# Attention and gated feed-forward block: the last row tile split as 384 and 128 columns, two scale sums over 64 columns

## The chip, the cores and the metric

One core of one Trainium2 chip runs the whole program. The metric is the device time of one execution in microseconds (us). The profile's span counts from the first to the last instruction and comes out some 2 us below the device time of the same run (776.1 beside 778.0 before). Before the prediction, the kernel before had a median of 777.64 us (3 runs, 777.15 to 778.16).

## The reference, cut to what matters

```python
x = A_x                                              # 2048 x 1024, bf16
h = x + _A_ref(_layernorm(x), A_wqkv, A_wo)           # 32 heads, sliding dilated window of 8, then wo
h2 = h + _B_ref(_layernorm(h), w_gate, w_up, w_down)  # ((ln @ w_gate) * (ln @ w_up)) @ w_down, width 3584
```

Nearly all the work is matrix products. The kernel computes some of them from sums and differences of sub-blocks, in fp16, with scales taken from sums of absolute values.

## The kernel before

The change touches two places. The first is the sum over partitions from which a scale is made: a matmul with a matrix of ones adds up the 128 partitions and broadcasts the total. The right-hand operand is one column repeated 512 times, and only column 0 of the result is read.

```python
def total(self, ps=None):
    ps = ps or psum.tile([128, TC], F32, tag="mm", name="l1ps" + self.name)      # TC = 512
    nc.tensor.matmul(ps[:], lhsT=ones[:], rhs=self.rowb[:].to_broadcast((128, TC)), start=True, stop=True)
    tot = const.tile([128, 1], F32, name="tot" + self.name)
    nc.vector.tensor_copy(tot[:], ps[:, 0:1])
    ...                                                    # four small VectorE steps make the scale
```

It is called four times. The scales `d` and `gu` take a bank of their own (`ps` is None); `h1` and `h` are given a bank.

The second place is the end of the kernel: four row tiles `q` of 128 rows by 512 columns. `dprod` is 14 pairs of weight load and matmul onto a bank that already holds a partial result. `result` scales, adds and stores.

```python
for q in range(4):
    if q < 3:
        dprod(ps_y[q], q, HF["12"], fcells(down["b22"]), False)
        result(2, hs2[q], q, 1, ps_y[q], inv, p5[q])
        if q == 0:
            nc.scalar.copy(ps_x[0][:, 256:512], ps_y[3][:, 256:512])
    else:
        for ps, lo in ((ps_y[3], 0), (ps_x[0], 256)):
            dprod(ps, q, HF["12"], fcells(down["b22"]), False, lo, 256)
            result(2, hs2[q], q, 1, ps, inv, p5[q], lo, 256)
```

The last tile is done in two column groups in two banks, so that the first half is evicted and stored while TensorE computes the second.

Of the kernel before, what the change touches and what calls it, by code (L numbers as in the profile page):

```python
# [25 lines left out]
TC = 512  # L26
# [52 lines left out]
def kernel(  # L79
# [11 lines left out]
    nc = tc.nc  # L91
# [441 lines left out]
    ones = const.tile([128, 128], BF)  # L533
    nc.vector.memset(ones[:], 1.0)

    class Scale:
# [11 lines left out]
            nc.vector.tensor_copy(self.rowb[:], row[:])  # L548

        def total(self, ps=None):  # L550
            ps = ps or psum.tile([128, TC], F32, tag="mm", name="l1ps" + self.name)
            nc.tensor.matmul(ps[:], lhsT=ones[:], rhs=self.rowb[:].to_broadcast((128, TC)), start=True, stop=True)
            tot = const.tile([128, 1], F32, name="tot" + self.name)
            nc.vector.tensor_copy(tot[:], ps[:, 0:1])
            eb = const.tile([128, 1], I32, name="eb" + self.name)
            nc.vector.tensor_scalar(eb[:], tot[:].bitcast(I32), 0x7F800000, None, ALU.bitwise_and)
            nc.vector.tensor_scalar(eb[:], eb[:], float(27 << 23), None, ALU.max)
            sb = const.tile([128, 1], I32, name="sb" + self.name)
            nc.vector.tensor_scalar(sb[:], eb[:], -1.0, float(266 << 23), ALU.mult, ALU.add)
            ib = const.tile([128, 1], I32, name="ib" + self.name)  # L560
            nc.vector.tensor_scalar(ib[:], eb[:], float(12 << 23), None, ALU.subtract)
            self.s, self.inv = sb[:].bitcast(F32), ib[:].bitcast(F32)
# [200 lines left out]
    def f16(ap):  # L763
        return ap.bitcast(F16)
# [19 lines left out]
    def fcells(homes):  # L784
        return [f16(t[:, k, :]) for t in homes for k in range(NH)]

    def dprod(ps, q, lhs, rhs, fresh, lo=0, n=TC):
        for k in range(NP):
            nc.tensor.matmul(ps[:, bass.ds(lo, n)], lhsT=lhs[k][:, bass.ts(q, 128)], rhs=rhs[k][:, bass.ds(lo, n)],  # L789
                             start=(fresh and k == 0), stop=(k == NP - 1), skip_group_check=not fresh)  # L790

    def result(c, rows, t, hf, ps, sc, other, lo=0, n=TC):
        cols = bass.ds(hf * 512 + lo, n)
        nc.vector.scalar_tensor_tensor(rows[:, cols], ps[:, bass.ds(lo, n)], sc,
                                       rows[:, cols] if other is None else other[:, bass.ds(lo, n)], ALU.mult, ALU.add)
        nc.sync.dma_start(outf[bass.ds(c * TC + t * 128, 128), cols], rows[:, cols])
# [124 lines left out]
    hs2 = hss[2]  # L921
# [84 lines left out]
    down = {}  # L1006
# [28 lines left out]
    ps_x = [psum.tile([128, TC], F32, tag="mm", name=f"dx{q}") for q in range(4)]  # L1035
    ps_y = [psum.tile([128, TC], F32, tag="mm", name=f"dy{q}") for q in range(4)]
# [6 lines left out]
    for q in range(4):  # L1043
        dprod(ps_x[q], q, HA["11"], fcells(down["b11"]), True)
        if q == 1:
            scale_h.total(ps_y[3])
            inv = const.tile([128, 1], F32, name="inv_hd")
            nc.vector.tensor_tensor(inv[:], scale_h.inv, scale_d.inv, ALU.mult)
            inv = inv[:]
# [3 lines left out]
    HF = {k: [f16(a) for a in HA[k]] for k in HA}  # L1053
# [22 lines left out]
    p5 = []  # L1076
# [24 lines left out]
    for q in range(4):  # L1101
        if q < 3:
            dprod(ps_y[q], q, HF["12"], fcells(down["b22"]), False)
            result(2, hs2[q], q, 1, ps_y[q], inv, p5[q])
            if q == 0:
                nc.scalar.copy(ps_x[0][:, 256:512], ps_y[3][:, 256:512])
        else:
            for ps, lo in ((ps_y[3], 0), (ps_x[0], 256)):
                dprod(ps, q, HF["12"], fcells(down["b22"]), False, lo, 256)
                result(2, hs2[q], q, 1, ps, inv, p5[q], lo, 256)  # L1110

# [1 line left out]
_INS = ['A_x', 'A_wqkv', 'A_wo', 'B_x', 'B_w_gate', 'B_w_up', 'B_w_down']  # L1113
# [26 lines left out]
```

## Time and profile before

| | before |
|---|---|
| median of the runs | 777.64 us |
| span of the profiled run | 776.1 us |
| TensorE busy | 770.0 us, 99% |
| one sum over 512 columns, on the chain | 0.21 us |
| last tile: first matmul to end of last eviction | 773.35 - 769.61 = 3.74 us |
| end of last eviction to end of span | 776.07 - 773.35 = 2.72 us |

The chain of work that ended last is read backwards from the last instruction: what stands on it sets the end. TensorE is 86% of it, so for most of the span a matmul's slot counts in full. At the very end the chain leaves TensorE: one eviction on VectorE and one store, with nothing beside them. The prediction shows the lines. The page rounds the span to 0.1 us; where 0.1 us matters below, the end is taken to 0.01 us from the view `--windows` (776.07 here).

### The profile page before, as it was taken

How to read it: one execution, taken by the hardware profiler on the slowest of the kernel's cores; microseconds unless marked ns; L12 is line 12 of the kernel's file. 1: busy time of each engine (PE TensorE's matmuls, PEld its weight loads, DVE VectorE, ACT ScalarE, POOL GpSimd, SP SyncE). 2: the span in 40 equal slices, each digit the busy share in tenths (PEclk: the TensorE clock that was granted, in tenths of full speed). 3: DMA queues.
4: the chain of work that ended last, by engine and by line, in shares of the span. 5: the costliest groups of instructions: out<-in, count | busy, mean ns of one | idle time of the engine just before them, and what ended most of it. 6: DMA issues, size and time to landing. Idle time of an engine off the chain costs nothing.

```text
span 776.1 us, 10428 instructions
## 1 busy us (share of the span) xinstructions
PE 770.0 (99%) x3691; PEld 354.4 (46%) x3691; DVE 612.0 (79%) x782; ACT 471.6 (61%) x1021; POOL 142.5 (18%) x152
## 2 busy tenths in 40 slices
PE   9999999999999999999999999999999999999998
PEld 6444444444444444444444444444444444444444
DVE  5619999999899999999988989985553444578862
ACT  4627445323476661975869889746677776788240
POOL 0000000020000200002000001008778687600000
PEclk9999999999999999999999999999999999999999
DMA  8999693895965869877745384644332423740001
GB/s 275 272 233 222 158 285 94 250 280 151 332 223 165 262 227 248 260 234 227 242 135 194 132 296 124 156 103 110 107 94 70 109 59 105 242 138 28 0 28 55
DMA packets 183716, 134.38 MB, mean 173 GB/s; under 512 B 81136, under 2 KB 176496, under 8 KB 181616
## 3 DMA queue, kind: packets, MB, share of 16 engines
q1 hardware_dynamic: 176912, 110.12, 50.5%
q0 software_dynamic: 3584, 22.02, 8.2%
q10 hardware_dynamic: 3168, 1.57, 0.8%
q8 instruction: 29, 0.48, 0.3%
q14 instruction: 23, 0.19, 0.1%
HBM read 104.86 MB, written 22.02 MB: 163 GB/s over the span
## 4 chain that ended last, share of the span: by engine, by line
PE 86%; DVE 9%; DMA 2%; ACT 1%; SPq 1%; issue 0%; ACTq 0%; DVEq 0%
PE ps L394 18%; PE pu L394 12%; PE pg L394 12%; PE dx L789 6%; PE pz L682 6%; PE acc L628 6%; PE py L682 6%; PE px L682 6%; PE wo L515 4%; PE pv L682 3%; PE dy L789 3%; DMA x<-in_A_x_dram 1%; DVE st L181 1%; DVE h L836 1%; DMA w_qkv<-in_A_wqkv_dram 1%; PE ps L355 1%
## 5 line engine op out<-in xcount | busy, mean ns | idle before, releaser
L394 PE MATMUL ps<-lnT,w_qkv 128*128 128x512 bf16 x736 | 159.7, 379 | 0.7 <-ACT sg L307 0.7
L394 PEld LDWEIGHTS <-w_qkv 128*128 128x128 bf16 x736 | 71.9, 98 | 87.0 <-issue 1.0
L394 PE MATMUL pg<-lnT,w_wg 128*128 128x512 bf16 x448 | 105.8, 379 | 0.0
L394 PE MATMUL pu<-lnT,w_wu 128*128 128x512 bf16 x448 | 105.8, 379 | 0.0
L307 ACT CAST sg<-ps 128x512 bf16<-128x512 f32 x96 | 54.8, 590 | 51.2 <-PE ps L394 48.5
L477 DVE TENSOR_TENSOR pv<-vD,at 128x4096 bf16<-128x4096 bf16 x32 | 72.5, 2286 | 0.3
L434 DVE TENSOR_TENSOR prod<-qD,kD 128x4096 bf16<-128x4096 bf16 x32 | 72.3, 2283 | 0.1
L682 PEld LDWEIGHTS <-sw 128*128 128x128 f16 x448 | 43.8, 98 | 53.5 <-issue 0.9
L394 PEld LDWEIGHTS <-w_wu 128*128 128x128 bf16 x448 | 43.8, 98 | 52.9
L394 PEld LDWEIGHTS <-w_wg 128*128 128x128 bf16 x448 | 43.8, 98 | 52.9
L598 ACT CAST us<-pu 128x512 bf16<-128x512 f32 x56 | 33.2, 593 | 40.5 <-PE pu L394 40.4
L682 PE MATMUL px<-lnT,ws 128*128 128x512 bf16 x224 | 55.2, 379 | 0.0
L682 PEld LDWEIGHTS <-ws 128*128 128x128 f16 x336 | 32.9, 98 | 39.6
L628 PE MATMUL acc<-w_wd,gs 128*128 128x512 bf16 x224 | 48.5, 379 | 0.0
L489 POOL DMA_DIRECT2D od<-oD x4 | 2.2, 544 | 251.7 <-DVE oD L487 162.5
L663 POOL TENSOR_TENSOR sw<-ws 128x512 f16<-128x512 f16 x26 | 30.0, 1154 | 84.6 <-PE py L682 77.3
L185 ACT ACTIVATE rs<-mv,eps 128x1 f32<-128x1 f32 (+1 forms) x25 | 7.4, 297 | 53.9 <-DVE mv L182 49.0
L593 ACT CAST gs<-pg 128x512 bf16<-128x512 f32 x56 | 32.9, 587 | 10.8 <-PE pg L394 8.7
L436 DVE TENSOR_TENSOR prod<-prod 128x4096 bf16<-128x4096 bf16 x16 | 36.6, 2287 | 0.3
L543 ACT ACTIVATE junkd<-w_wd 128x512 bf16<-128x512 bf16 x56 | 34.3, 613 | 0.0
L628 PEld LDWEIGHTS <-gs 128*128 128x128 bf16 x224 | 21.9, 98 | 26.4
L699 ACT COPY py<-px 128x512 f32<-128x512 f32 x28 | 16.0, 570 | 26.3 <-PE px L682 26.3
(312 smaller groups left out, 1393.4 us busy)
## 6 DMA issues: line engine op xcount, KB each, us to landing
w_wg<-in_B_w_gate_dram SPq DMA_DIRECT2D x14, 1024.0 KB, 6.7
w_wu<-in_B_w_up_dram SPq DMA_DIRECT2D x14, 1024.0 KB, 5.6
w_wd<-in_B_w_down_dram SPq DMA_DIRECT2D x8, 896.0 KB, 8.1
w_pair<-in_B_w_gate_dram SPq DMA_DIRECT2D x14, 512.0 KB, 4.0
w_pair<-in_B_w_up_dram SPq DMA_DIRECT2D x14, 512.0 KB, 5.2
w_wo<-in_A_wo_dram SPq DMA_DIRECT2D x6, 1024.0 KB, 8.3
w_qkv<-in_A_wqkv_dram SPq DMA_DIRECT2D x5, 1024.0 KB, 10.5
kd<-sg SPq DMA_DIRECT2D x32, 144.0 KB, 3.5
```

Source lines behind the costliest of these rows:

```text
L307: nc.scalar.copy(sg[:, HB:HB + TC], ps[:])
L394: nc.tensor.matmul(ps[:], lhsT=wt[:, ko, bass.ts(j, 128)], rhs=rhs[:, ko, :], start=(ko == 0), stop=(ko == KO - 1))
L434: nc.vector.tensor_tensor(prod[:, j], qD[:], kD[:, :, o:o + SUB], ALU.mult)
L436: nc.vector.tensor_tensor(prod[:, :, 0:16], prod[:, :, 0:16], prod[:, :, 16:32], ALU.add)
L477: nc.vector.tensor_tensor(pv[:, j], vD[:, :, o:o + SUB], at[:, w, None, :].to_broadcast((128, DH, SUB)), ALU.mult)
L515: nc.tensor.matmul(ps[:], lhsT=oTs[c][:, kk, t, :], rhs=wts["wo", c, hf][:, kk, :], start=(kk == 0), stop=(kk == KO - 1))
L543: nc.scalar.activation(junk, src, ACTF.Abs, accum_out=self.l1[:, k:k + 1])
L593: nc.scalar.copy(gs[:], pg[:])
L598: nc.scalar.copy(us[:], pu[:])
L628: nc.tensor.matmul(acc[t][:], lhsT=hT[f][:, bass.ts(t, 128)], rhs=wts["wd", c, hf, b][:, j, :], start=(f == 0), stop=(f == NF - 1))
L682: nc.tensor.matmul(ps[:], lhsT=lhs[:, ko, :], rhs=rhs[:, ko, :], start=(fresh and ko == 0), stop=(ko == 3), skip_group_check=not fresh)
L789: nc.tensor.matmul(ps[:, bass.ds(lo, n)], lhsT=lhs[k][:, bass.ts(q, 128)], rhs=rhs[k][:, bass.ds(lo, n)], start=(fresh and k == 0), stop=( ...
```

## The change

It is meant to shorten two sums of which one column is used, and to shorten the eviction and the store behind the last matmul by making the last column group smaller, at no cost in matmul columns. The diff, whole:

```diff
         def total(self, ps=None):
+            n = TC if ps else 64
             ps = ps or psum.tile([128, TC], F32, tag="mm", name="l1ps" + self.name)
-            nc.tensor.matmul(ps[:], lhsT=ones[:], rhs=self.rowb[:].to_broadcast((128, TC)), start=True, stop=True)
+            nc.tensor.matmul(ps[:, 0:n], lhsT=ones[:], rhs=self.rowb[:].to_broadcast((128, n)), start=True, stop=True)
@@
             if q == 0:
-                nc.scalar.copy(ps_x[0][:, 256:512], ps_y[3][:, 256:512])
+                nc.scalar.copy(ps_x[0][:, 384:512], ps_y[3][:, 384:512])
         else:
-            for ps, lo in ((ps_y[3], 0), (ps_x[0], 256)):
-                dprod(ps, q, HF["12"], fcells(down["b22"]), False, lo, 256)
-                result(2, hs2[q], q, 1, ps, inv, p5[q], lo, 256)
+            for ps, lo, n in ((ps_y[3], 0, 384), (ps_x[0], 384, 128)):
+                dprod(ps, q, HF["12"], fcells(down["b22"]), False, lo, n)
+                result(2, hs2[q], q, 1, ps, inv, p5[q], lo, n)
```

One line is added in `total`, so source lines after it are one higher in the profiles of the changed kernel (L552 is L553 there, L794 is L795).

## The prediction

> **What bounds the kernel now.** I read the page of the kernel before first, for the engines' busy shares and the chain that ended last, then the chain piece by piece around the two places where the diff acts (the sums over `ones`, and the last row tile), then the order in time of the last seven microseconds.
>
> ```profile
> PE 770.0 (99%) x3691; PEld 354.4 (46%) x3691; DVE 612.0 (79%) x782; ACT 471.6 (61%) x1021; POOL 142.5 (18%) x152
> PEclk9999999999999999999999999999999999999999
> PE 86%; DVE 9%; DMA 2%; ACT 1%; SPq 1%; issue 0%; ACTq 0%; DVEq 0%
> ```
>
> TensorE is busy for 770.0 of 776.1 us at the full granted clock (1.000 in the list of cores), and the chain that ended last runs for 86% of its time through TensorE. So a saved TensorE issue slot is worth its own length, as long as the chain passes through it. The chain in order of time says so for both changed sums; the columns are start in us, length in us, and what:
>
> ```profile
> 390.35 1.73 PE pu L394 x8
> 392.07 0.21 PE l1psd L552
> 392.29 1.73 PE pg L394 x8
> ...
> 453.59 1.73 PE wo L834 x8
> 455.31 0.21 PE l1psgu L552
> 455.53 1.73 PE wo L834 x8
> 457.25 0.22 PE ey L552
> 457.47 1.74 PE wo L834 x8
> 459.21 0.02 issue
> 459.23 0.69 DVE h L836
> ```
>
> Each sum is one matmul of 0.21 us, directly between its neighbours, with no wait on either side. At 459.23 us the chain passes to VectorE, and it is TensorE that releases VectorE there. Until 521.81 us the chain then runs through VectorE and ScalarE, mostly.
>
> The end of the kernel, in order of time (start, length from first start to last end, engine, line, operation):
>
> ```profile
> 769.61 0.82 PE L789 MATMUL dy<-dn_b22a,hq 128*128 128x256 f16 x6
> 769.81 0.75 DVE L794 SCALAR_TENSOR_TENSOR h<-dy,inv_hd,dp 128x512 bf16<-128x512 f32 x1 [2.27 <-PE dy L789]
> ...
> 771.14 0.82 PE L789 MATMUL dx<-dn_b22a,hq 128*128 128x256 f16 x6
> 771.41 0.48 DVE L794 SCALAR_TENSOR_TENSOR h<-dy,inv_hd,dp 128x256 bf16<-128x256 f32 x1 [0.84 <-PE dy L789]
> ...
> 772.45 0.38 PE L789 MATMUL dx<-dn_b22b,kx 128*128 128x256 f16 x2
> 772.87 0.48 DVE L794 SCALAR_TENSOR_TENSOR h<-dx,inv_hd,dp 128x256 bf16<-128x256 f32 x1 [0.98 <-PE dx L789]
> 773.38 0.33 SPq L796 DMA_DIRECT2D out_dram<-h  x1
> ```
>
> The last row tile is two groups of 14 matmuls of 256 columns. After the last matmul nothing is hidden: eviction (0.48 us), issue of the store at 773.38, its landing (1.6 us from issue for the 64 KB stores), and the closing work up to 776.1. The first half's eviction and store lie beside the second half's matmuls.
>
> **What the Trainium skill says, and whether this trace agrees.** (1) TensorE: Matmul & The Clock Gate, section Back-to-back issue gap, gives N/2.4 + 2.5 ns as the isolated gap of a warm matmul of N columns, and about 81 ns at N=128 and 131 ns at N=512 for a sustained stream of weight load and matmul pairs. The trace agrees with the formula where it can be checked: 14 pairs of 512 take 769.61 - 766.59 = 3.02 us, 215.7 ns each; 14 pairs of 256 take 771.14 - 769.61 = 1.53 us, 109.3 ns each (formula 109.2). It contradicts the 131 ns. (2) Same page, Single matmul latency: (398 + N)/2.4 ns warm. The groups show 379 ns at 512, 272 at 256 and 219 at 128, as the formula says; an end of a matmul is modelled, though. (3) VectorE: DVE Perf Modes, section The TRN2 errata, charges a fixed term plus one 0.96 GHz cycle per column for an fp32 PSUM source. The slope agrees (751 - 483 = 268 ns for 256 columns, 1.047 ns each); the fixed term here is larger (215 ns against 125). (4) DMA: Bandwidth & Descriptors, Specifications: below 512 B a transfer is a read-modify-write. The new last store has 256 B rows. No isolated store of that shape is in the trace, so this stays open.
>
> **The change part by part.** The instruction order of both kernels was compared: every engine keeps the same sequence and waits; only the column counts differ. Nothing is added or moved between engines.
>
> *Two sums.* `total` without a given bank is called for the `d` and `gu` scales; the `h1` and `h` sums are given a bank and keep 512 columns. So two matmuls go from 512 to 64 columns. The formula gives 64/2.4 + 2.5 = 29 ns (an estimate from the skill's page above), but then the next pair's weight load might set the pace. What this core has shown for short pairs is in the first microseconds, at 128 columns and clock 1.00:
>
> ```profile
> 9.20 0.61 PE L349 MATMUL pt<-ident,ln 128*128 128x128 bf16 x8
> 9.65 2.11 PE L355 MATMUL ps<-lnT,w_qkv 128*128 128x128 bf16 x32
> ```
>
> Subtracting one matmul's 219 ns: (2.11 - 0.219)/31 = 61 ns per pair, and (0.61 - 0.22)/7 = 56 ns. So a pair can go at 56 ns with a 98 ns load under it; the spacing at 64 columns should lie between 29 and 61. I take 45: each sum saves 216 - 45 = 171 ns, two save 0.34 us. The first shifts everything on TensorE after 392; VectorE waits for TensorE at the `wo` additions (the longest such wait before 459 is 1.24 us), so the shift is handed over at 459.23, and from there to 521.81 VectorE carries it. A constant earlier start of all of it keeps the 0.34.
>
> *Last tile, TensorE.* Group one: 14 x (384/2.4 + 2.5) = 14 x 162.5 = 2.275 us. Group two: 13 gaps of 58 ns (my choice between 56 and 61) and one end of 219 ns = 0.973. Last result at 769.61 + 2.275 + 0.973 = 772.86. Before, worked out in the same way: 769.61 + 14 x 0.1093 + 13 x 0.1093 + 0.272 = 772.83. Cost: +0.03 us (0.00 to +0.07 for 56 to 61).
>
> *Last tile, VectorE.* The last eviction has 128 columns: 483 - 128 x 1.047 = 349 ns, saving 0.13 us on the path. The other, of 384 columns, takes 483 + 134 = 617 ns. Its group's last matmul starts at 769.61 + 13 x 0.1625 = 771.72 and ends 326 ns later, so with the 0.11 us seen today between an end and an eviction it runs from about 772.16 to 772.78. The last eviction may start at 772.90: clear by 0.12 us.
>
> *Stores.* First store issued at about 772.81 (96 KB), second at about 773.28 (32 KB) instead of 773.38; one issue takes 0.33 us, so they don't collide. From issue to landing the trace has 1.7 us for 128 KB and 1.6 for 64 KB: bytes hardly count, and I give the halved last store 0.00 (within -0.05 and +0.1).
>
> *The bank copy* on ScalarE shrinks from 256 to 128 columns, off the path (ScalarE is idle at the end): 0.
>
> Sum: -0.34 + 0.03 - 0.13 + 0.00 = -0.44 us. Because some of the handover at 459 may be lost, I take -0.40: 777.64 - 0.40 = 777.24 us.
>
> **The rivals.** *Weight loads set the pace of short matmuls.* Loads are 98 ns each; if two could not overlap, group two would be 13 x 98 + 219 = 1.49 us, the tail +0.55 - 0.13 = +0.42, and the sums would save only 2 x 118 ns = 0.24: net +0.18, 777.8 us. The skill's 81 ns lies between (13 x 81 + 219 = 1.27, tail +0.20, sums -0.27: about -0.07, 777.6). Against both: the 56 and 61 ns of the fence above.
>
> *The sums' gain doesn't arrive.* VectorE or ScalarE could be the real bound between 392 and 521, a load or transpose coming last there, so that TensorE only waits longer later. Then only the tail's -0.10 remains: 777.5 us. For it: from 459 the chain is VectorE's for 60 us, and ScalarE's conversions (busy until 458.43 before the 458.72 step) leave only 0.3 us of slack there. Against it: VectorE idles for TensorE three times just before.
>
> *The first, larger half becomes the last.* If its 617 ns eviction or its store holds up the last one, the gain of the shorter last eviction is eaten: about +0.1, 777.35 us. The worked margin of 0.12 us is thin, but positive.
>
> *Small rows.* If 256 B rows cost a read-modify-write at the end, the last landing takes perhaps 0.1 us longer (an estimate: the whole data phase of such a store is a fraction of its 1.6 us): 777.35 us.
>
> **Range and chances.** All mechanisms lie between -0.5 and +0.2 us, which is under 0.07% of the time. The three runs of before spread over 1.01 us (777.15 to 778.16), so a median of a few runs is itself uncertain by some 0.3 to 0.4 us, and more than the change is worth is noise. That gives 776.6 to 778.0 for 8 in 10. A 2% change is 15.6 us; nothing here is of that size. Faster by over 2%: 0.003; within: 0.994; slower: 0.003.
>
> **What would show each step right or wrong.** In the changed kernel's profile: the chain should show `l1psd` and `l1psgu` at 0.03 to 0.06 us instead of 0.21; the span between the start of the last 512-column group and the last eviction should grow by 0.00 to 0.07; the last eviction should be near 349 ns and the one before near 617; the store's landing should stay at 1.5 to 1.7 us; the span should fall from 776.1 to about 775.7. A spacing near 98 ns in the 128-column group would make the weight load rival right; an unchanged time of the first `pv` product near 521.81 would mean that the sums' gain was absorbed. The prediction as a whole is wrong if the time moves by more than 1 us, for example by a different settling of the transfers in the middle.

## The result, and the profile after

The changed kernel took 776.76 us (median of 5 runs, 776.52 to 777.62), the kernel before 778.16 us (5 runs, 777.15 to 778.51). The ratio is 0.9988, with a 95% interval of 0.9973 to 1.0002: the same within 2%, and no change at all is inside the interval. A ratio here is the mean time of one kernel's runs over that of the other's of the same rounds, so it is not quite the ratio of the medians that are quoted.

The profiled run's span fell from 776.1 to 774.8 us. Its page:

```profile
PE 768.9 (99%) x3691; PEld 353.5 (46%) x3691; DVE 612.0 (79%) x782; ACT 471.3 (61%) x1021; POOL 142.1 (18%) x152
...
PE 86%; DVE 9%; DMA 2%; ACT 1%; SPq 1%; issue 0%; DVEq 0%
```

What bounds the kernel is as before. The chain in order of time around the two sums (start, length, what):

```profile
391.42 0.03 PE l1psd L553
391.45 1.73 PE pg L394 x8
...
454.47 0.03 PE l1psgu L553
454.50 1.73 PE wo L835 x8
456.23 0.22 PE ey L553
...
458.20 0.69 DVE h L837
```

Each changed sum has shrunk from 0.21 to 0.03 us. `ey`, which keeps 512 columns, still takes 0.22. The `h` addition on VectorE, which started at 459.23, starts at 458.20, 1.03 us sooner. Two sums account for 0.36 us of that. The rest was there before the first of them: `l1psd` starts at 391.42 instead of 392.07, 0.65 us sooner, although nothing ahead of it was changed. I come to that below.

The end in order of time:

```profile
768.60 1.14 PE L790 MATMUL dy<-dn_b22a,hq 128*128 128x384 f16 x6
...
770.88 0.50 PE L790 MATMUL dx<-dn_b22a,hq 128*128 128x128 f16 x6
771.14 0.62 DVE L795 SCALAR_TENSOR_TENSOR h<-dy,inv_hd,dp 128x384 bf16<-128x384 f32 x1 [1.59 <-PE dy L790]
...
771.54 0.28 PE L790 MATMUL dx<-dn_b22b,kx 128*128 128x128 f16 x2
771.86 0.35 DVE L795 SCALAR_TENSOR_TENSOR h<-dx,inv_hd,dp 128x128 bf16<-128x128 f32 x1
```

From the first matmul of the last tile to the end of the last one it takes 771.54 + 0.28 - 768.60 = 3.22 us, as before (772.45 + 0.38 - 769.61 = 3.22). The spacing in the 128-column group is (0.50 - 0.219)/5 = 56 ns. The eviction of 384 columns ends at 771.76, 0.10 us before that of 128 columns begins. The last eviction takes 0.35 instead of 0.48 us, and from its end at 772.21 to the end of the span it takes 2.64 us instead of 2.72. The view `--windows`, with the restart near 60 us that is explained below; the columns are the window, its length, then busy times, first in the kernel before, then in the changed one:

```profile
60.39:776.07 715.68, 712.06 (x3310) 323.76 (x3309) 582.50 (x718) 444.83 (x943) 139.46 (x134) 1.00 0.56 166
773.35:776.07 2.72, 0.00 (x0) 0.00 (x0) 0.00 (x1) 0.00 (x0) 0.00 (x0) 1.00 0.08 24
```

```profile
59.74:774.85 715.11, 711.69 (x3310) 323.14 (x3309) 582.48 (x718) 444.59 (x943) 139.24 (x134) 1.00 0.56 165
772.21:774.85 2.64, 0.00 (x0) 0.00 (x0) 0.00 (x0) 0.00 (x0) 0.00 (x0) 1.00 0.17 50
```

The stores of the last microseconds, from issue to landing (median us in the last column), after:

```profile
out_dram<-h SPq DMA_DIRECT2D x1, 96.0 KB, 1.6
out_dram<-h SPq DMA_DIRECT2D x1, 32.0 KB, 1.5
```

Before, the two stores of 64 KB took 1.6 us. So the smaller store with its 256 B rows lands sooner, not later.

**Where 0.65 us of the 1.22 came from.** TensorE waits for a ScalarE copy near 60 us: 0.7 us before, 0.2 after. The chain there, first in the kernel before, then in the changed one (the view was cut at 64 us, and so was the count of matmuls in each last line):

```profile
45.83 9.14 DMA x<-in_A_x_dram
...
60.39 3.61 PE ps L394 x16
```

```profile
45.55 8.76 DMA x<-in_A_x_dram
...
59.74 4.48 PE ps L394 x20
```

Behind the load of `x` stand its statistics on VectorE and a square root step on ScalarE; the copies out of PSUM queue up on ScalarE behind that step, and TensorE goes on when they have been done, at 60.39 or at 59.74 us. From there to the end it takes 776.07 - 60.39 = 715.68 us before and 774.85 - 59.74 = 715.11 us after. So 0.65 us of the difference belongs to the first 60 us, and 0.57 to the rest, where both edits are. I call these two parts the first part and the rest. The expectations below were written from spans rounded to 0.1 us, which gave 715.71, 715.06 and so 0.65 us for the rest; the tables and the text here use the spans to 0.01 us.

### The profile page after: what moved, and what is told of

The parts are those of the page before. It is cut to its first block, busy times and chain, and to the rows that moved or that the text cites. A ratio compares the mean times of both kernels' runs of the same rounds, so it can differ in the third digit from the quotient of the medians.

```text
span 774.8 us, 10428 instructions
## 1 busy us (share of the span) xinstructions
PE 768.9 (99%) x3691; PEld 353.5 (46%) x3691; DVE 612.0 (79%) x782; ACT 471.3 (61%) x1021; POOL 142.1 (18%) x152
## 4 chain that ended last, share of the span: by engine, by line
PE 86%; DVE 9%; DMA 2%; ACT 1%; SPq 1%; issue 0%; DVEq 0%
PE ps L394 18%; PE pu L394 12%; PE pg L394 12%; PE dx L790 6%; PE pz L683 6%; PE acc L629 6%; PE py L683 6%; PE px L683 6%; PE wo L515 4%; PE pv L683 3%; PE dy L790 3%; DMA x<-in_A_x_dram 2%; DVE st L181 1%; DVE h L837 1%; PE ps L355 1%; PE ex L790 1%
```

## The experiments

My theory (A): the change is worth what the rest shows (0.57 us; 0.65 as first read), and the first part is chance. Rivals: the first part's gain belongs to the change as well (B); the sums' gain is partly absorbed later (C); small rows cost at the end (D). Eleven kernels ran in three groups, each beside the kernel before on the same chip, all with a correct result. The table has the profiles' two parts and the timed means of nine of them; late_stats and best, in which the restart is gone, come at the end.

| kernel | first part | rest | mean time less the mean of before beside it (ratio, 95%) |
|---|---|---|---|
| before | 60.39 | 715.68 | |
| changed | 59.74 | 715.11 | 776.99 - 777.95 = -0.96 (0.9988) |
| changed, again | 60.84 | 715.09 | -0.40 (0.9995, 0.9982 to 1.0007) |
| null | 60.16 | 715.66 | -0.13 (0.9998, 0.9984 to 1.0011) |
| sums_only | 60.39 | 715.28 | -0.22 (0.9996, 0.9984 to 1.0009) |
| tail_only | 60.19 | 715.45 | -0.15 (0.9997, 0.9985 to 1.0010) |
| four_sums | 60.00 | 714.70 | -1.04 (0.9986, 0.9973 to 0.9998) |
| rep17_512 | 59.79 | 722.80 | median +6.51 (1.0112, 1.0060 to 1.0164) |
| rep17_64 | 60.37 | 716.30 | +0.34 (1.0005, 0.9990 to 1.0020) |
| tail_448_64 | 59.96 | 715.48 | -0.56 (0.9993, 0.9978 to 1.0008) |
| tail_whole | 59.86 | 715.74 | -0.64 (0.9993, 0.9976 to 1.0010) |

### The same kernel twice: null and after_again

The edit of null is a comment; after_again is the changed kernel, not edited.

```diff
-GROUP_US = 1.73
+GROUP_US = 1.73  # unchanged
```

> The kernel before with one comment added. It measures what two measurements of the same program differ by. Both theories expect a ratio of 1.000; the question is the size of the chance part. Theory A (the change is worth about 0.65 us, the rest of the measured difference is chance from the first 60 us, where input loads set the pace): the span counted from the restart of the qkv matmuls after the wait for the third x tiles (60.39 us in the profile before, 59.74 in the profile after) to the end is 715.7 us within 0.1, whatever the part before that point takes, and that part differs from 60.39 by several tenths. Rival B (the whole 1.3 us between the two profiled runs belongs to the change): the first part comes at 60.4 within 0.1.

> The changed kernel once more, beside before and the two others on one chip. Theory A: the change is worth 0.65 us, so the mean lies 0.4 to 0.9 us below before, and the first measurement's 0.96 us (means) was partly chance; the span after the restart near 60 us is 715.06 within 0.1. Rival B: again 1.0 to 1.4 us.

Null: the rest 715.66, beside before's 715.68, and the first part 60.16 instead of 60.39. (Its expectation calls the `x` tiles the third, counted from 0; they are the fourth block.) The changed kernel again: the rest 715.09, beside 715.11 at first, but the first part 60.84 instead of 59.74. Its chain there:

```profile
46.25 9.16 DMA x<-in_A_x_dram
...
60.84 3.18 PE ps L394 x14
```

The same program differed from itself by 1.10 us ahead of the restart, and by 0.02 us behind it, which is also what before and null differ by. This time the changed kernel was 0.40 us below before, not 0.96; theory A had expected 0.4 to 0.9. Rival B falls: the first part belongs to the runs, not to the change.

### Each half alone: sums_only and tail_only

sums_only has only the hunk in `total`, tail_only only the hunk in the last tile.

```diff
-            nc.tensor.matmul(ps[:], lhsT=ones[:], rhs=self.rowb[:].to_broadcast((128, TC)), start=True, stop=True)
+            n = TC if ps else 64
+            nc.tensor.matmul(ps[:, 0:n], lhsT=ones[:], rhs=self.rowb[:].to_broadcast((128, n)), start=True, stop=True)
```

```diff
-            for ps, lo in ((ps_y[3], 0), (ps_x[0], 256)):
+            for ps, lo, n in ((ps_y[3], 0, 384), (ps_x[0], 384, 128)):
```

> The kernel before with only the two 64-column sums. Theory A: each of the two sums takes 0.03 us on the chain instead of 0.21, so the span after the restart near 60 us is 715.71 - 0.37 = 715.34, within 0.1; the time is 0.4 us below before, hardly clear of the noise. Rival C (VectorE or a load absorbs the shift after 459 us): that span is 715.5 to 715.7. Rival B: the first 60 us shorten as well, though none of the edit stands there.

> The kernel before with only the 384 and 128 columns. Theory A: the last eviction is 0.13 us shorter, the store lands 0.1 us sooner, TensorE takes the same, so the span after the restart near 60 us is 715.71 - 0.29 = 715.42, within 0.1 (this and sums_only together make the 0.65 of the changed kernel); time 0.2 to 0.3 us below before, inside the noise. Rival D (the store's rows of 256 B cost a read-modify-write that shows at the end): from the end of the last eviction to the end of the span it takes longer than the 2.75 us of before.

The rest is 715.28 with the sums alone (-0.40) and 715.45 with the tail alone (-0.23). Together that is 0.63, and the changed kernel has 0.57 and 0.59 in its two traces: the halves add up to within 0.06. In tail_only the last eviction ends at 773.01 and the span at 775.64, 2.63 us later. In all traces with a last store of 64 KB this stretch is 2.71 or 2.72 us (before, null, sums_only, rep17_512, rep17_64), and with the 32 KB store of 256 B rows it is 2.63 or 2.64 (changed twice, tail_only, four_sums): rival D, a cost on balance, falls. The timed means (-0.22 and -0.15) have intervals that include no change; timing alone would have shown nothing.

### The disputed cost, seventeen times: rep17_512 and rep17_64

```diff
+            r, n = (1, TC) if ps else (17, TC)        # rep17_64: (17, 64)
             ps = ps or psum.tile([128, TC], F32, tag="mm", name="l1ps" + self.name)
-            nc.tensor.matmul(ps[:], lhsT=ones[:], rhs=self.rowb[:].to_broadcast((128, TC)), start=True, stop=True)
+            for _ in range(r):
+                nc.tensor.matmul(ps[:, 0:n], lhsT=ones[:], rhs=self.rowb[:].to_broadcast((128, n)), start=True, stop=True)
```

> The kernel before with the sums for the d and gu scales computed 17 times over each in the same bank (same result), 512 columns. Enlarges the disputed cost far above the noise: 32 more matmuls. Theory A (every slot at both places is worth its own length): 32 x 0.2157 = +6.9 us. Rival C (a shift of TensorE at 392 or 455 us is absorbed later): +3.5 us or less.

> The same 17 repetitions with 64 columns. If the column count alone sets the spacing (64/2.4 + 2.5 = 29 ns) then 17 of them take 0.49 us and the time is 2 x (0.49 - 0.216) = +0.6 us over before. If a weight load of 98 ns that cannot overlap another sets the pace of short matmuls: 17 x 98 = 1.67 us each, +2.9 us. In between (56 to 61 ns, what pairs of 128 columns show): +1.5 us. The spacing within the 17 is read from the trace.

With 512 columns the rest grew by 722.80 - 715.68 = 7.12 us, the median by 6.51 (784.71 beside 778.20; one of the four runs took 793.41, for which no trace was kept, so I don't use the mean; the ratio in the table still contains it). Expected was 6.9, and 3.5 or less had either place absorbed it. Rival C falls. With 64 columns the rest grew by 0.62, as expected from the column count (0.6), not by 1.5 or 2.9. The chain of rep17_64:

```profile
392.05 0.53 PE l1psd L554 x17
...
455.59 0.53 PE l1psgu L554 x17
```

That is 0.53/17 = 31 ns for a pair of weight load and matmul, although each load is recorded with 98 ns: in these two stretches of 17 the loads overlap, and 98 ns is not the pace of matmuls of 64 columns.

### Other splits of the last tile: tail_448_64 and tail_whole

Both keep the two 64-column sums. In tail_whole the last tile is one group of 512. The bank copy goes with the split (columns 448 to 512, or none); it is left out here.

```diff
-            for ps, lo, n in ((ps_y[3], 0, 384), (ps_x[0], 384, 128)):
+            for ps, lo, n in ((ps_y[3], 0, 448), (ps_x[0], 448, 64)):      # tail_448_64
+            for ps, lo, n in ((ps_y[3], 0, TC),):                          # tail_whole
```

> The changed kernel with the last row tile as 448 and 64 columns. Tests the rival of the prediction that the larger first half gets in the way. Theory: the first eviction takes 215 + 448 x 1.047 = 684 ns and starts 2.91 us after the group's first matmul, so it ends at 3.60; the second group's last result is there at 3.25, so the last eviction (282 ns) waits 0.35 us for VectorE and ends 0.28 us later than in the changed kernel, counted from the first matmul of the last tile (3.61 there, 3.88 here). If the 64-column pairs go at 29 ns the trace shows 14 in about 0.57 us; at 56 ns 0.92 us, and then VectorE is still the one that comes last. Time about 0.2 to 0.3 us above the changed kernel, inside the noise; the trace decides.

> The changed kernel with the last row tile in one piece of 512 columns, as the other tiles. What the split itself is worth: TensorE ends at the same time (14 x 215.7 ns = 3.02, plus the end), the eviction takes 0.75 us instead of 0.35 and the store of 128 KB lands at 1.7 instead of 1.5 us. From the last tile's first matmul to the end 0.5 to 0.7 us longer than in the changed kernel; 0.3 longer than in the kernel before. Should it be no longer, the split does nothing and the 0.13 us of the prediction falls.

The end of tail_448_64 in order of time:

```profile
768.82 1.30 PE L790 MATMUL dy<-dn_b22a,hq 128*128 128x448 f16 x6
...
771.74 0.68 DVE L795 SCALAR_TENSOR_TENSOR h<-dy,inv_hd,dp 128x448 bf16<-128x448 f32 x1 [1.97 <-PE dy L790]
771.82 0.22 PE L790 MATMUL dx<-dn_b22b,kx 128*128 128x64 f16 x2
772.34 0.28 DVE L795 SCALAR_TENSOR_TENSOR h<-dx,inv_hd,dp 128x64 bf16<-128x64 f32 x1
772.45 0.81 SPq L797 DMA_DIRECT2D out_dram<-h  x2
```

TensorE is done at 772.04, but the last eviction begins only at 772.34, when the first one is nearly out (772.42). It ends 772.62 - 768.82 = 3.80 us after the tile's first matmul (expected 3.88; the changed kernel 3.61). Then the span goes on for 2.82 us instead of 2.64, though the store is smaller still. The second issue alone, in tail_448_64 and then in the changed kernel:

```profile
772.87 0.38 SPq L797 DMA_DIRECT2D out_dram<-h  x1
```

```profile
772.24 0.36 SPq L797 DMA_DIRECT2D out_dram<-h  x1
```

In tail_448_64 it begins 0.25 us after its data were ready (772.62), and 0.42 us after the first issue (772.45). In the changed kernel it begins 0.03 us after its data (772.21), as in the kernel before (773.38 beside 773.35), and 0.45 us after the first issue (771.79). So the queue went from one issue to the next in 0.42 us at the least, and the changed kernel had some 0.03 us to spare. At 448 columns the larger group is in the way twice, on VectorE (read from the trace) and, as these times suggest, on the store queue: this rival of the prediction is true at 448 columns and not at 384. The rest is 715.48, 0.37 worse than the changed kernel.

In tail_whole the last eviction runs from 771.95 for 0.75 us and the span ends at 775.60, 2.90 us after it. The rest is 715.74, 0.63 worse than the changed kernel (expected 0.5 to 0.7) and 0.46 worse than sums_only with its 256 and 256. With before and after this gives the time from the end of the last eviction to the end of the span by the size of the last store: 2.90 us at 128 KB, 2.72 at 64 KB, 2.64 at 32 KB.

The timed means of these two (-0.56 and -0.64) lie below what the profiles' rest gives (-0.20 and 0.06). Their intervals include both, and the first parts of the two profiled runs are 0.43 and 0.53 us shorter than that of before; whether more than chance is in it stays open.

### All four sums: four_sums

```diff
-            n = TC if ps else 64
+            n = 64
```

> The changed kernel with all four sums at 64 columns. Theory A: two more matmuls go from 0.216 to 0.03 us. The one at 457 us lies on the chain, so 0.18; the one at 693 us lies in a stretch that is TensorE's before and passes to VectorE at 713 us, which has its own start from this sum, so 0.0 to 0.18. Span after the restart near 60 us: 715.06 - 0.18 to 0.37 = 714.7 to 714.9; time 0.8 to 1.1 us below before. Rival C: 715.06, nothing more to be had.

The rest is 714.70, 0.41 less than the changed kernel (0.39 less than its second trace): both further sums gave their full 0.18, which is 0.36 in all. Timed, this version was 1.04 us below before (medians 776.84 and 777.88; means the same 1.04), with an interval of 0.9973 to 0.9998 that leaves out no change. It beats the kernel before, and by the trace the changed kernel too, though the two were not timed in the same group.

### Where the first part's chance comes from: late_stats and best

Both schedule the statistics of the fourth block of `x` later; best has the four sums and the 384 and 128 columns as well.

```diff
-    bg.add(stats_gen(norm1[3]), bg.now + 6.0)
+    bg.add(stats_gen(norm1[3]), bg.now + 14.0)
```

> The kernel before, with the statistics of the fourth x block scheduled later (ready 14 us instead of 6 us after the point where they are queued; one number). It tests where the chance part of the first 60 us comes from. In all ten profiles TensorE waits once near 60 us for a ScalarE copy (0.2 to 0.7 us), and the chain before that wait goes back to the load of x (8.5 to 9.1 us): ScalarE, in order, sits in a square root step until x has landed, and the copies out of PSUM stand behind it. Theory A: with the step behind more copies, that wait disappears from the list of TensorE's waits, the first part shortens by 0.2 to 0.7 us, and the run to run spread shrinks. Rival E: the chance comes from the launch and the first loads alone (matmuls of 512 columns start at 17.0 to 17.5 us); then the spread stays, and moving the attention's VectorE work may cost time later.

> All four sums at 64 columns, 384 and 128 columns in the last tile, and the later statistics. Theory A: 1.0 us from sums and tail (715.71 - 714.70, measured in four_sums) plus 0.2 to 0.7 us at 60 us: 1.2 to 1.7 us below before, ratio near 0.998. Rival E: about 1.0 us, as four_sums.

The theory was right on the wait and wrong on the time. TensorE's wait near 60 us is gone in both, which shows that the place of these statistics, with the square root step at their end, had caused it. But the kernels took 785.09 and 784.90 us (medians; ratios 1.0091 and 1.0087), 7 us more. TensorE's waits in late_stats begin with

```profile
PE wo L834 <- ACT ep L932: 6.0, 1, 6.0
```

The attention is dealt out in pieces between the other VectorE work, and the one number changed the dealing, far from where it stands: the four attention outputs were issued to their stores at 146.79, 249.70, 352.35 and 453.82 us before, and at 146.69, 248.32, 357.03 and 457.30 in late_stats. The chain then runs through the last of these stores and a weight load behind it, and TensorE waits 6.0 us for a ScalarE step that comes after. It starts again at 488.76 us at a lower granted clock, which is 1.000 on average in the kernel before; two windows of late_stats (the clock is the third number from the end; it is 1.00 again from 492):

```profile
488.00:490.00 2.00, 1.24 (x4) 0.40 (x4) 2.00 (x10) 2.00 (x4) 0.00 (x0) 0.50 0.02 4
490.00:492.00 2.00, 2.00 (x7) 0.76 (x6) 1.47 (x8) 1.94 (x5) 0.00 (x0) 0.57 0.00 0
```

The first seven matmuls after the wait start 381 to 427 ns after one another in the trace, instead of 216: some 1.4 us more, which with the 6.0 and less the 0.7 near 60 us is nearly all of the 7. Which piece was dealt otherwise, I did not trace. On the spread the runs say nothing clear: 784.85 to 786.06 in late_stats, 784.78 to 785.15 in best.

## Why the prediction was right or wrong

As a whole it was right: 776.76 lies in 776.6 to 778.0, and the class was "within 2%". The point 777.24 was 0.48 us too high, and that distance is mostly chance: the median moved 0.88 us from the 777.64 that the prediction started from, of which the change is 0.57 by the traces, and the second measurement of the same kernel gave 777.58. Its sign of danger, a move of more than 1 us, did come up between the medians of the same rounds (1.40), and the repetition put it down: the change is 0.57 and 0.59 us by two traces, the rest chance.

- **The two sums, -0.34.** Right: 2 x (0.21 - 0.03) = 0.36 on the chain, 0.40 in sums_only. The guess of 45 ns was too careful; the pairs went at 31 ns. The 61 ns in the prediction is a misreading: its group of 32 matmuls has one pause of 222 ns after the eighth (10.04 to 10.26 us), and all its other spacings are 55 or 56 ns.
- **Some of it lost at 459 us, +0.04.** Wrong, but small. Nothing was lost: the 1.03 us by which 458.20 is sooner (0.65 of it from the first part) was still 1.02 at the first `pv` product (520.79 after, 521.81 before), and rep17_512 passed on all of a far larger shift.
- **TensorE in the last tile, +0.03.** The 56 ns end of my range held, not the 58 I took: 0.00 (3.22 us before and after).
- **The last eviction, -0.13.** Right: 0.48 to 0.35 us. The margin to the larger eviction, worked out as 0.12, was 0.10. That the two stores don't collide came true with less room than thought: the prediction reckoned with 0.33 us for an issue, and tail_448_64 shows 0.42 from one to the next.
- **The stores, 0.00.** This is the term that was most mis-sized, though little: "bytes hardly count, and I give the halved last store 0.00 (within -0.05 and +0.1)". Measured: -0.08 from the end of the last eviction (2.72 to 2.64 us), just outside that range, and the same in tail_only. The landing medians of 1.7 and 1.6 us had shown a step of 0.1 per halving, and I rounded it away, out of respect for the small rows.
- **The span would fall to about 775.7.** It fell to 774.85. With the first part of before it would have been 60.39 + 715.11 = 775.50.

The sum by its own steps, as measured: -0.36 + 0.00 - 0.13 - 0.08 = -0.57 us, which is what the rest shows. The mechanism was right, and the -0.40 was too small by the store (0.08), the allowance at 459 (0.04), the last tile on TensorE (0.03) and the pace of the sums (0.02).

The rivals: weight loads as the pace of short matmuls fell (rep17_64, 31 ns); absorption fell (rep17_512); the larger half in the way is not so at 384 columns but is at 448 (tail_448_64); small rows, as a cost on balance, fell (tail_only).

## What to carry to other kernels

When an engine is on the chain nearly all the time, a slot saved on it counts in full, and can be added up from the chain's own rows; but an effect under 0.1% is read from a fixed point of the trace behind the chance part, and not from a few timed runs. At the end of a kernel, split the last tile so that the last piece is small, but stop where the eviction and the store issue of the larger piece are still finished when the small one is ready: of the splits tried here that was 384 and 128 columns, not 448 and 64. A small stall is not free to remove: moving one background task by 8 us to save 0.7 us cost 7, some 1.4 of it in matmuls that started again at a lower granted clock.

## What the Trainium skill lacked or had wrong

- TensorE: Matmul & The Clock Gate, Back-to-back issue gap: for a stream of weight load and matmul pairs it gives about 81 ns at 128 columns and 131 at 512, and says that the plain formula under-counts at small N. Here unbroken runs of pairs followed N/2.4 + 2.5 ns: 56 ns at 128 columns (last tile after), 215.7 at 512, and 31 at 64 columns (17 in 0.53 us; formula 29).
- DMA: Bandwidth & Descriptors, Specifications: it says that transfers below 512 B are read-modify-writes. No cost of that was seen in a last store of 128 rows of 256 B: it landed in 1.5 us, the one with 512 B rows in 1.6.
- The same page has a formula of a transfer's time by its bytes for the path over GpSimd alone, and none for a small store issued by SyncE, as here. From the end of the last eviction to the end of the span these runs show 2.90, 2.72 and 2.64 us for 128, 64 and 32 KB.
- VectorE: DVE Perf Modes, The TRN2 errata: the fixed term for a PSUM source is some 125 ns there; the evictions here, which read a second tensor beside the PSUM source, have some 218 (351 ns at 128 columns and 751 at 512, so 1.042 ns per column).
